# Products of phi(K) and V on eight small tiles of the matrix engine, with the memory kept as two heads per partition

## The chip, the cores and the metric

One core of a Trainium2 chip runs the kernel. The metric is the time of one execution on the device in microseconds (us). TensorE (PE in the profile) multiplies matrices into PSUM banks; VectorE (DVE), ScalarE (ACT) and GpSimd (POOL) work element by element; SyncE (SP) issues the transfers. Each engine works through a queue of its own, in order, and waits on semaphores for the others.

## The reference

Two branches work on the same input x (2048 rows of 512) and are mixed by a gate. Branch A is an attention with a compressive memory: 32 heads of 16 dimensions, four segments of 512 rows. Branch B is a gated feed-forward layer of width 1792.

```python
for s in range(N):                       # N = 4 segments, L = 512 rows each
    qs, ks, vs = q[:, :, s], k[:, :, s], v[:, :, s]
    p = softmax(einsum('bhqd,bhkd->bhqk', qs, ks) * scale + mask)
    a_dot = einsum('bhqk,bhkd->bhqd', p, vs)
    pq = phi(qs)                         # phi(t) = t + 1 for t > 0, else exp(t)
    num = einsum('bhld,bhde->bhle', pq, M)
    den = einsum('bhld,bhd->bhl', pq, z)[..., None] + 1e-06
    outs.append(g * num / den + (1.0 - g) * a_dot)
    pk = phi(ks)
    M = M + einsum('bhld,bhle->bhde', pk, vs)
    z = z + einsum('bhld->bhd', pk)
a = concat(outs) @ wo
b = (gelu(x @ w_gate) * (x @ w_up)) @ w_down
out = gate * a + (1 - gate) * b          # gate = sigmoid(sum(x * gate_w))
```

The memory M of a head is a 16x16 matrix and z a vector of 16; the program carries them together as 17 columns, since V is stored with a column of ones behind each head's 16.

## The kernel before

Everything is laid out by one program text that emits the instructions of all engines in order. The attention goes by blocks i = 8 heads of one segment (four chunks c per segment, 16 blocks in all). A block is visited several times, 72 visits in all (written `visits`). A visit emits the scores of one or two 64-key pieces (`group_qk`, L638: 4 or 8 matmuls on tiles of 32 rows by 128 columns), the exponential of the whole four-bank score tile on ScalarE (L643), and the mask of the diagonal on GpSimd (L647). Only one score tile exists, so the scores of the next visit wait for the exponential of this one. When all pieces of a block are there, `lump` emits the sum of values `pv` (L663): 128 loads and matmuls on eight tiles of 64 rows by 32 columns into two banks called od, which VectorE transposes out (L670) and later normalizes.

Between the scores of two visits TensorE is filled with units of the other work: projections k, q, v (L376, L290, L414), gate, up and down of branch B (L473, L494, L510), the output product (L527), and the memory. The units stand in streams; a planner (`fill_to`) picks the next one by its due visit and by VectorE's backlog, and adds up booked times: `t_pe` for TensorE, `t_act` for ScalarE. `left()` sums the booked TensorE times of units still to come, and the slack that follows from it is spread over the visits. A unit ends with the evacuation of its PSUM bank by VectorE or ScalarE. All these units and od share a pool of four banks (`gen`); `room_for_bank` finishes an open unit once two more banks have been taken.

The memory runs through these steps for each of the first three segments:

- `u_pk` (L406): a transposing transfer from SyncE turns phi(K) of a chunk so that the 512 keys stand on partitions (tile pk).
- `u_M` (L540): a unit, twice per segment, each for two chunks. For a chunk and each of four groups of 128 keys a full 128x128 load of pk is multiplied with V of all eight heads of the chunk, 8 x 17 = 136 columns (L548), into tile MT. So all 64 pairs of heads in a chunk are computed, of which the eight on the diagonal are used. VectorE adds MT to Macc (L555): 128 partitions (head and dimension) by 4 chunks by 8 heads by 17.
- `u_mask` (L559): a product with the block mask bm makes the bf16 tiles Mz (the denominators' part, L572) and Mn (L561, in two halves, two and eight visits later) of the next segment.
- `u_den` (L580, tile zd) and `mem_num` (L613, tile mn) multiply phi(Q) with them.

The units of the memory stand in one stream M, with due visits:

```python
us += [unit(u_M(s, half), NP * s + 10 + 2 * half, ("M", s),
            lambda s=s: count(("pk", s)) == NC8 and clock[0] >= pk_at[s] + 3)
       for half in range(2)]
us.append(unit(u_mask(s + 1), 0))
```

The turned keys of the next segment are written over the old ones, so `u_pk` of segment s + 1 waits for both halves of segment s. At the end a test of the inputs' size either leaves the result or runs `general()`, a slower safe path that the inputs here don't take.

Of the kernel before, what the change touches and what calls it, by code (L numbers as in the profile page):

```python
# [11 lines left out]
ALU = mybir.AluOpType  # L12

P = 128
D = 512
H = 32
DH = 16
NSEG = 4
DFF = 1792
FC = D // P  # L20
NC8 = H // 8
# [7 lines left out]
NP = 2 * NV  # L29
# [3 lines left out]
F32 = dt.float32  # L33
# [20 lines left out]
def kernel(  # L54
# [15 lines left out]
    nc = tc.nc  # L70
    S = A_x.shape[1]
    L = S // NSEG
    KT = L // P
# [10 lines left out]
    def const(shape, dtype, name):  # L84
        return cpool.tile(shape, dtype, name=name, tag=name)
# [10 lines left out]
    bm = const([P, 8, 17], BF, "bm")  # L96
# [1 line left out]
    beta = const([P, H], BF, "beta")  # L98
    gh = const([P, H], F32, "gh")
    og = const([P, H], F32, "og")  # L100
    Macc = const([P, NC8, 8, 17], F32, "Macc")
    Mn = [const([P, NC8, 128], BF, f"Mn{i}") for i in range(2)]
    Mz = [const([P, NC8, 8], BF, f"Mz{i}") for i in range(2)]
    rdm = [const([P, KT, H], F32, f"rdm{i}") for i in range(2)]
# [20 lines left out]
    def gen(name):  # L125
        return pgen.tile([P, 512], F32, name=name, tag="gen")
# [200 lines left out]
    def count(key):  # L327
        return done.get(key, 0)
# [208 lines left out]
            return MM512  # L537
        return 4 * MM512, EVAC, f

    def u_M(s, half):  # L540
        def f():
            T = gen("MT")
            Tv = T[:, 0:272].rearrange("p (c h e) -> p c h e", c=2, h=8)
            Tm = T[:, 0:272].rearrange("q (c j p e) -> q c j p e", c=2, j=4, p=2)
            for cc in range(2):
                c = 2 * half + cc
                for kt in range(KT):
                    nc.tensor.matmul(Tm[:, cc], lhsT=pk[:, kt, c * P:(c + 1) * P],  # L548
                                     rhs=Vh[s % 2][:, kt, :, 4 * c:4 * c + 4, 0:17]
                                     .rearrange("q p j e -> q j p e"),  # L550
                                     start=(kt == 0), stop=(kt == KT - 1))
                if cc == 0:
                    yield 0.3
            mv = Macc[:, 2 * half:2 * half + 2, :, :]
            nc.vector.tensor_tensor(out=mv, in0=mv, in1=Tv, op=ALU.add)  # L555
            return 0.3
        return 0.6, 0.4, f

    def u_mask(s):  # L559
        def half(h0):  # L560
            nc.vector.tensor_tensor(  # L561
                out=Mn[s % 2][:, h0:h0 + 2, :].rearrange("p c (h e) -> p c h e", h=8),
                in0=Macc[:, h0:h0 + 2, :, 0:16],
                in1=bm[:, None, :, 0:16].to_broadcast((P, 2, 8, 16)), op=ALU.mult)
            passed(0.0, 0.78)
            done["Mn", s] = count(("Mn", s)) + 1

        def f():
            if general_now[0]:
                half(0)  # L570
                half(2)
            nc.vector.tensor_tensor(out=Mz[s % 2][:, :, :], in0=Macc[:, :, :, 16],  # L572
                                    in1=bm[:, None, :, 16].to_broadcast((P, NC8, 8)),
                                    op=ALU.mult)
            if not general_now[0]:
                later(2, lambda: half(0))
                later(8, lambda: half(2))
        return 0.0, 0.2, f
# [123 lines left out]
    def unit(u, want, key=None, when=None):  # L702
        return u + (key, when, want)
# [8 lines left out]
    def passed(pe, dve=0.0):  # L712
        backlog[0] = max(0.0, backlog[0] - pe) + dve
        t_pe[0] += pe
# [18 lines left out]
    def room_for_bank():  # L733


        if current:
            current[0][3][0] += 1
            while current and current[0][3][0] > 2:
                step()
# [42 lines left out]
    def run(u):  # L782
        if u[0] == 0.0:
            u[2]()
        else:
            for _ in u[2]():
                pass
# [65 lines left out]
    us = []  # L853
    for s in range(NSEG - 1):
        us += [unit(u_pk(s, c), 0, ("pk", s), lambda s=s, c=c: ("k", s, c - c % 2) in ready
                    and (s == 0 or count(("M", s - 1)) == 2)) for c in range(NC8)]
    streams.append(Stream("T", us))

    def u_x3():
# [9 lines left out]

    us = []  # L870
    for s in range(NSEG - 1):
        us += [unit(u_M(s, half), NP * s + 10 + 2 * half, ("M", s),
                    lambda s=s: count(("pk", s)) == NC8 and clock[0] >= pk_at[s] + 3)
               for half in range(2)]
        us.append(unit(u_mask(s + 1), 0))
        us += [unit(u_den(s + 1, pair), NP * s + 16 + 9 * pair, ("den", s + 1),
                    lambda s=s, pair=pair: ("q", s + 1, 2 * pair) in ready)
               for pair in range(2)]
# [43 lines left out]
    def lump(i):  # L922
        s, c = i // NC8, i % NC8
        assert count(("vs", s)) == 1
        oT = oTs[s]
        o2 = wk2.tile([P, 16, 2, DH], BF, name="o2", tag="o2")
        room_for_bank()
        room_for_bank()
        oq = pv(s, c, blocks.pop(i))
        passed(PV_T, 1.44)  # L930

        def f_norm(p):
            norm(c, p, oq[p], o2)
            passed(0.0, 0.76)

        def f_back():
            back(c, o2, oT)
            passed(0.0, 0.7)
            if s == 0:
                later(1, f_ready)  # L940

        def f_add():
            assert (s, c) in tms
            add_mem(s, c, oT)
            passed(0.0, 0.43)
            later(1, f_ready)

        def f_ready():
            done["tr", s] = count(("tr", s)) + 1
        later(1, lambda: f_norm(0))  # L950
        later(2, lambda: f_norm(1))
        later(3, f_back)
        if s > 0:
            later(4, f_add)
# [131 lines left out]
    def general():  # L1086
        general_now[0] = True
        queue[0] = nc.gpsimd
        nc.gpsimd.memset(Macc[:, :, :, :], 0.0)
        nc.vector.tensor_copy(hm[:, :], bm[:, :, 16])  # L1090
        for s in range(NSEG):
            oT = wk2.tile([P, FC, L], BF, name="oT", tag="oT")
            oTs[s] = oT
            if s % NX == 0:
                rows = G[(s + 1) % NG][:, 0:KT, :]
                nc.gpsimd.dma_start(rows, x2[s * L:(s + 1) * L, :]
                                    .rearrange("(k p) d -> p k d", p=P))
                for fc in range(FC):
                    turn(xS[s % NX][:, fc, :].rearrange("p (k t) -> p k t", k=KT),
                         rows[:, :, fc * P:(fc + 1) * P])  # L1100
            for c in range(NC8):
                run(u_k(s, c))
                run(u_q(s, c))
            for kt in range(KT):
                run(u_v(s, kt))
            run(u_vz(s))
            run(u_vs(s))
            if s > 0:
                for c in range(0, NC8, 2):
                    phi_now(pq[:, c:c + 2, :], QT[:, c:c + 2, :])  # L1110
                run(u_mask(s))
                run(u_den(s, 0))
                run(u_den(s, 1))
            neg = G[(s + 1) % NG][:, 8, 0:P]
            nc.gpsimd.memset(neg, 0.0)
            nc.gpsimd.affine_select(out=neg, in_=neg, pattern=[[-1, P]], compare_op=ALU.is_ge,
                                    fill=-1e9 * DH ** 0.5, base=0, channel_multiplier=1)
            for c in range(NC8):
                o2 = wk2.tile([P, 16, 2, DH], BF, name="o2", tag="o2")
                if s > 0:  # L1120
                    mem_num(s, c)
                tiles = {}
                for b in range(5):
                    t = ptp.tile([P, 4, 512], BF, name="pT", tag="pT")
                    tiles[b] = (t, 0)
                    if 1 <= b <= 3:
                        tiles[NB - b] = (t, L - 64 * b)
                general_blocks(s, c, tiles)
                oq = pv(s, c, tiles)
                for p in range(2):  # L1130
                    norm(c, p, oq[p], o2)
                back(c, o2, oT)
                if s > 0:
                    add_mem(s, c, oT)
            for hs in range(HS):
                run(u_gate(s, hs, False))
            gelu(s)
            for hs in range(HS):
                run(u_up(s, hs))
            for qt in range(KT):  # L1140
                run(u_down(s, qt))
            for qt in range(KT):
                run(u_out(s, qt))
            if s < NSEG - 1:
                for c in range(0, NC8, 2):
                    phi_now(ktb[:, c:c + 2, :], ktb[:, c:c + 2, :])
                for c in range(NC8):
                    run(u_pk(s, c))
                for half in range(2):
                    run(u_M(s, half))  # L1150

    flag = nc.alloc_registers("safe", engines=[mybir.EngineType.PE, mybir.EngineType.DVE,
                                               mybir.EngineType.Activation,
# [36 lines left out]
```

## Time and profile before

| what | before |
|---|---|
| median of 3 runs (269.92 to 272.15) | 269.92 us |
| the profiled execution | 269.92 us |
| its span, first to last instruction | 268.2 us |
| mean granted TensorE clock | 0.999 of full speed |
| visits of the attention | 28.1 us (first scores) to 251.4 us (end of the last exponential) |
| the six pieces of u_M start at | 57.2, 62.8, 118.9, 127.2, 190.3, 196.1 us |

A page of the profile gives for each engine its busy time, its share of the span and its number of instructions. A row of a group gives the source line, the engine, the operation, output and inputs with their shapes (partitions x elements) and the count; behind the bar stand the busy time in all (us), the mean of one (ns), and the engine's idle time just before them with what ended it. Matmuls overlap, so a matmul's mean is its latency, and its cost is the distance from its start to the next one's. PEld are weight loads. A list of waits gives: who waited, for whom, us in total, how often, the longest. In order of time a row gives the start (us), the duration (us), engine, line, and the number of instructions merged.

### The profile page before, as it was taken

To read this page: it belongs to the slowest core of one execution; us is meant where nothing else is said; L and a number is where in the kernel's file an instruction comes from. 1 tells how busy PE (TensorE), PEld (TensorE's weight loads), DVE (VectorE), ACT (ScalarE), POOL (GpSimd) and SP (SyncE) were. 2 spreads that over 40 slices of the span, in tenths; PEclk is the share of its full clock that TensorE was granted. 3 is DMA by queue.
4 is the path that set the end of the run, shared out by engine and by line. 5 is a ranking of instruction groups with operands and counts; after the bars stand their busy time and mean duration, and the time that the engine had idled before them with its cause. 6 is when DMAs were issued, how large, how long until landed. Compare 5 with 4: busy or idle time off the path is not lost.

```text
span 268.2 us, 6580 instructions
## 1 busy us (share of the span) xinstructions
PE 262.7 (98%) x2713; PEld 118.0 (44%) x2713; DVE 204.0 (76%) x391; ACT 209.0 (78%) x163; POOL 156.9 (58%) x298
## 2 busy tenths in 40 slices
PE   7999999999999999999999999999999999999994
PEld 3454434344454444544444444434454544344441
DVE  2999575968778787697985979686889479698364
ACT  3236889999997998889999988889888987657510
POOL 4000158897905979987921998596785079655500
PEclk9999999999999999999999999999999999999999
DMA  6999911200070000301032001100000200003102
GB/s 213 304 197 329 341 36 39 42 4 0 20 145 2 0 22 22 78 4 42 0 61 62 4 21 42 42 20 22 20 24 21 66 2 20 2 20 42 40 22 83
DMA packets 30281, 16.59 MB, mean 62 GB/s; under 512 B 20008, under 2 KB 28968, under 8 KB 30248
## 3 DMA queue, kind: packets, MB, share of 16 engines
q1 hardware_dynamic: 30248, 16.14, 23.4%
q8 instruction: 22, 0.36, 0.6%
q14 instruction: 11, 0.09, 0.1%
HBM read 8.14 MB, written 2.10 MB: 38 GB/s over the span
## 4 chain that ended last, share of the span: by engine, by line
PE 87%; POOL 5%; issue 4%; DMA 2%; ACT 1%; SPq 0%; DVE 0%; ACTq 0%; DVEq 0%; POOLq 0%
PE gT L473 19%; PE uT L494 17%; PE dT L510 14%; PE lg L638 8%; PE od L663 6%; PE aT L527 5%; PE qT L290 5%; PE kT L376 5%; PE vT L414 4%; POOL pT L647 3%; POOL KTm L386 2%; DMA wk<-in_A_wk_dram 2%; PE MT L548 1%; PE mn L617 1%; ACT pT L643 1%
## 5 line engine op out<-in xcount | busy, mean ns | idle before, releaser
L647 POOL TENSOR_SCALAR_AFFINE_SELECT pT<-pT 64x256 bf16<-64x256 bf16 x256 | 113.9, 445 | 94.3 <-ACT pT L643 81.5
L643 ACT ACTIVATE pT<-lg 128x2048 bf16<-128x2048 f32 x72 | 135.1, 1876 | 24.9 <-PE lg L638 21.6
L494 PE MATMUL uT<-x,wup 128*128 128x512 bf16 x224 | 60.4, 380 | 0.0
L473 PE MATMUL gT<-x,wga 128*128 128x512 bf16 x224 | 57.0, 380 | 0.0
L510 PE MATMUL dT<-wdn,G 128*128 128x512 bf16 x224 | 52.9, 380 | 0.0
L500 DVE TENSOR_TENSOR G<-uT,G 128x512 bf16<-128x512 f32 x56 | 38.1, 684 | 6.4 <-PE uT L494 6.2
L386 POOL TENSOR_SCALAR KTm<-ktb,eo 128x512 bf16<-128x512 bf16 x26 | 40.6, 1571 | 1.3
L670 DVE STREAM_TRANSPOSE oq<-od 128x512 f32<-128x512 f32 x32 | 21.0, 695 | 19.3 <-PE od L663 19.3
L510 PEld LDWEIGHTS <-G 128*128 128x128 bf16 x224 | 20.8, 98 | 25.0 <-issue 2.1
L473 PEld LDWEIGHTS <-wga 128*128 128x128 bf16 x224 | 20.4, 98 | 23.9 <-issue 2.2
L494 PEld LDWEIGHTS <-wup 128*128 128x128 bf16 x224 | 19.8, 97 | 24.0 <-issue 5.4
L638 PE MATMUL lg<-QT,KTm 32*128 32x192 bf16 (+7 forms) x512 | 28.6, 287 | 0.0
L313 DVE CAST G<-gT 128x512 bf16<-128x512 f32 x24 | 16.5, 688 | 9.7 <-PE gT L473 9.5
L638 PEld LDWEIGHTS <-KTm 32*128 32x128 bf16 x512 | 8.3, 92 | 28.3 <-issue 28.0
L663 PE MATMUL od<-pT,V 64*32 64x128 bf16 (+7 forms) x512 | 19.4, 284 | 0.2 <-POOL pT L647 0.2
L663 PE MATMUL od<-pT,Vs 64*32 64x128 bf16 (+7 forms) x512 | 19.4, 284 | 0.0
L488 ACT ACTIVATE G<-G 128x3584 bf16<-128x3584 bf16 x6 | 18.8, 3182 | 0.0
L676 DVE SCALAR_TENSOR_TENSOR o<-oq,ogs,rden 128x256 bf16<-128x256 f32 x32 | 17.0, 532 | 1.1
L376 PE MATMUL kT<-x,wk 128*128 128x512 bf16 x64 | 16.8, 380 | 0.7 <-DMA wk<-in_A_wk_dram 0.7
L290 PE MATMUL qT<-x,wq 128*128 128x512 bf16 x64 | 16.6, 379 | 0.0
L532 DVE SCALAR_TENSOR_TENSOR tB<-aT,gct,tB 128x512 bf16<-128x512 f32 x16 | 11.9, 746 | 6.0 <-PE aT L527 5.7
L527 PE MATMUL aT<-wo,oT 128*128 128x512 bf16 x64 | 16.5, 380 | 0.0
(96 smaller groups left out, 276.0 us busy)
## 6 DMA issues: line engine op xcount, KB each, us to landing
out_dram<-tB SPq DMA_DIRECT2D x16, 128.0 KB, 1.7
wup<-in_B_w_up_dram SPq DMA_DIRECT2D x1, 1792.0 KB, 8.7
wdn<-in_B_w_down_dram SPq DMA_DIRECT2D x1, 1792.0 KB
wga<-in_B_w_gate_dram SPq DMA_DIRECT2D x1, 1280.0 KB, 10.5
Vs<-V SPq DMA_DIRECT2D x8, 144.0 KB, 2.6
G<-in_A_x_dram SPq DMA_DIRECT2D x2, 256.0 KB, 2.8
wk<-in_A_wk_dram SPq DMA_DIRECT2D x2, 256.0 KB, 4.5
wq<-in_A_wq_dram SPq DMA_DIRECT2D x1, 512.0 KB, 5.8
```

Of the source, the lines that this page charges most:

```text
L290: nc.tensor.matmul(T[:, :], lhsT=wq[:, fc, c * P:(c + 1) * P], rhs=xS[s % NX][:, fc, :], start=(fc == 0), stop=(fc == FC - 1))
L376: nc.tensor.matmul(T[:, :], lhsT=wk[:, fc, c * P:(c + 1) * P], rhs=xS[s % NX][:, fc, :], start=(fc == 0), stop=(fc == FC - 1))
L386: eng.tensor_scalar(out=KTm[:, (NC8 * s + c) % NK, :, p, :], in0=ktb[:, c, :].rearrange("q (b k) -> q b k", b=NB), scalar1=eo[:, p:p + 1], ...
L473: nc.tensor.matmul(T[:, :], lhsT=wga[:, fc, hs * P:(hs + 1) * P], rhs=xS[s % NX][:, fc, :], start=(fc == 0), stop=(fc == FC - 1))
L494: nc.tensor.matmul(T[:, :], lhsT=wup[:, fc, hs * P:(hs + 1) * P], rhs=xS[s % NX][:, fc, :], start=(fc == 0), stop=(fc == FC - 1))
L500: nc.vector.tensor_tensor(out=g, in0=T[:, :], in1=g, op=ALU.mult)
L510: nc.tensor.matmul(T[:, :], lhsT=G[s % NG][:, hs, qt * P:(qt + 1) * P], rhs=wdn[:, hs, :], start=(hs == 0), stop=(hs == HS - 1))
L527: nc.tensor.matmul(T[:, :], lhsT=oT[:, fc, qt * P:(qt + 1) * P], rhs=wo[:, fc, :], start=(fc == 0), stop=(fc == FC - 1))
L638: nc.tensor.matmul(lg[:, j, off:off + n], lhsT=KTm[rows, i % NK, b].rearrange("r p k -> r (p k)"), rhs=QT[rows, i % NC8, 64 * b:L], start= ...
L643: nc.scalar.activation(pT[:, :, :], lg[:, :, :], AF.Exp, scale=DH ** -0.5)
L647: nc.gpsimd.affine_select(out=v, in_=v, pattern=[[0, 4], [1, 64]], compare_op=ALU.is_ge, fill=0.0, base=0, channel_multiplier=-1)
L663: nc.tensor.matmul(od[p][32 * j:32 * j + 32, 64 * b:L], lhsT=w[:, 18 * h:18 * h + 32], rhs=t[rows, j, off:off + n], start=(b == 0), stop=( ...
```

## The change

The unit u_M is gone. A function `memory(s)` does the products of a whole segment at once, on the eight 64x32 tiles that `pv` uses: tile column j of a chunk holds its heads 2j and 2j + 1 (32 partitions), tile row `half` holds 64 of the 128 keys. Each load is 64 keys by 32 columns of pk, each matmul has the 2 x 17 = 34 columns of the same two heads, and the two halves of the keys go to two banks. That makes 128 loads and matmuls per segment in place of 16 full ones. VectorE adds both banks to Macc, which now keeps two heads per partition (4 x 2 x 17 values). `u_mask` spreads them to the four pairs while it masks, chunk by chunk for Mn; Mz comes first in both paths. `memory` isn't a unit of a stream: `lump` calls it, when the keys are turned, just ahead of `pv`, after two more calls of `room_for_bank`, and books 0.5 us of TensorE and 0.6 us of VectorE for it.

```diff
-    Macc = const([P, NC8, 8, 17], F32, "Macc")
+    Macc = const([P, NC8, 2, 17], F32, "Macc")
...
-    def u_M(s, half):
-        def f():
-            T = gen("MT")
-            Tv = T[:, 0:272].rearrange("p (c h e) -> p c h e", c=2, h=8)
-            Tm = T[:, 0:272].rearrange("q (c j p e) -> q c j p e", c=2, j=4, p=2)
-            for cc in range(2):
-                c = 2 * half + cc
-                for kt in range(KT):
-                    nc.tensor.matmul(Tm[:, cc], lhsT=pk[:, kt, c * P:(c + 1) * P],
-                                     rhs=Vh[s % 2][:, kt, :, 4 * c:4 * c + 4, 0:17]
-                                     .rearrange("q p j e -> q j p e"),
-                                     start=(kt == 0), stop=(kt == KT - 1))
-                if cc == 0:
-                    yield 0.3
-            mv = Macc[:, 2 * half:2 * half + 2, :, :]
-            nc.vector.tensor_tensor(out=mv, in0=mv, in1=Tv, op=ALU.add)
-            return 0.3
-        return 0.6, 0.4, f
+    def memory(s):
+        Ts = [gen("MT") for half in range(2)]
+        for c in range(NC8):
+            for kt in range(KT):
+                for j in range(4):
+                    for half in range(2):
+                        rows = slice(64 * half, 64 * half + 64)
+                        nc.tensor.matmul(
+                            Ts[half][32 * j:32 * j + 32, 34 * c:34 * c + 34]
+                            .rearrange("q (p e) -> q p e", p=2),
+                            lhsT=pk[rows, kt, P * c + 32 * j:P * c + 32 * j + 32],
+                            rhs=Vh[s % 2][rows, kt, :, 4 * c + j, 0:17],
+                            start=(kt == 0), stop=(kt == KT - 1),
+                            tile_position=(64 * half, 32 * j))
+        for half in range(2):
+            nc.vector.tensor_tensor(
+                out=Macc[:, :, :, :], in0=Macc[:, :, :, :],
+                in1=Ts[half][:, 0:34 * NC8].rearrange("q (c p e) -> q c p e", c=NC8, p=2),
+                op=ALU.add)
+        done["M", s] = 1
 
     def u_mask(s):
         def half(h0):
+            for c in (h0, h0 + 1):
+                nc.vector.tensor_tensor(
+                    out=Mn[s % 2][:, c, :].rearrange("q (j p d) -> q j p d", j=4, p=2),
+                    in0=Macc[:, c, None, :, 0:16].to_broadcast((P, 4, 2, DH)),
+                    in1=bm[:, :, 0:16].rearrange("q (j p) d -> q j p d", j=4), op=ALU.mult)
+            passed(0.0, 0.6)
...
-                    and (s == 0 or count(("M", s - 1)) == 2)) for c in range(NC8)]
+                    and (s == 0 or count(("M", s - 1)) == 1)) for c in range(NC8)]
...
-        us += [unit(u_M(s, half), NP * s + 10 + 2 * half, ("M", s),
-                    lambda s=s: count(("pk", s)) == NC8 and clock[0] >= pk_at[s] + 3)
-               for half in range(2)]
-        us.append(unit(u_mask(s + 1), 0))
+        us.append(unit(u_mask(s + 1), 0, None, lambda s=s: count(("M", s)) == 1))
...
         room_for_bank()
         room_for_bank()
+        for z in range(NSEG - 1):
+            if (count(("M", z)) == 0 and count(("pk", z)) == NC8 and clock[0] >= pk_at[z] + 3):
+                room_for_bank()
+                room_for_bank()
+                memory(z)
+                passed(0.5, 0.6)
         oq = pv(s, c, blocks.pop(i))
```

## The prediction

> **What bounds the kernel now.** I read the busy times first, then TensorE's waits, then the groups of the lines that the change touches, then TensorE in order of time around the work that is moved.
>
> ```profile
> PE 262.7 (98%) x2713; PEld 118.0 (44%) x2713; DVE 204.0 (76%) x391; ACT 209.0 (78%) x163; POOL 156.9 (58%) x298
> ```
>
> ```profile
> PE warm L166 <- PEq L1174: 1.0, 1, 1.0
> PE kT L376 <- DMA wk<-in_A_wk_dram: 0.7, 1, 0.7
> PE od L663 <- POOL pT L647: 0.2, 1, 0.2
> ```
>
> The second fence is the whole list of TensorE's waits: 1.9 us, of which 1.7 lie in the first 7 us. A busy TensorE is not one at its peak, so I also looked at the distance from one matmul's start to the next: matmuls of 512 columns start 216 ns apart all through the span, and hardly anything lies between them. So TensorE's own queue sets the end: what the change takes from it or adds to it is paid nearly one to one, and what it does to other engines costs nothing until TensorE waits for it. The groups that matter (count, total and mean ns):
>
> ```profile
> L548 PE MATMUL MT<-V,pk 128*128 128x136 bf16 x48 | 4.1, 226 | 0.0
> L588 PE MATMUL zd<-Mz,pq 128*128 128x8 bf16 x48 | 2.2, 167 | 0.0
> L555 DVE TENSOR_TENSOR Macc<-Macc,MT 128x272 f32<-128x272 f32 x6 | 2.5, 422 | 0.0
> L561 DVE TENSOR_TENSOR Mn<-Macc,bm 128x256 bf16<-128x256 f32 x6 | 3.1, 518 | 0.0
> L572 DVE TENSOR_TENSOR Mz<-Macc,bm 128x32 bf16<-128x32 f32 x3 | 0.8, 283 | 0.1
> ```
>
> The mean of a matmul row is its latency, with its neighbours overlapped. Its price is the distance between starts, read from TensorE in order of time (start us, duration us):
>
> ```profile
> 62.83 0.68 PE L548 MATMUL MT<-V,pk 128*128 128x136 bf16 x8
> 63.35 0.38 PE L494 MATMUL uT<-x,wup 128*128 128x512 bf16 x1
> ...
> 75.64 0.34 PE L588 MATMUL zd<-Mz,pq 128*128 128x8 bf16 x8
> 75.84 1.24 PE L473 MATMUL gT<-x,wga 128*128 128x512 bf16 x5
> ```
>
> Eight MT matmuls take 63.35 - 62.83 = 0.52 us (by the trace's nanoseconds 0.51). Eight zd matmuls, of 8 columns only, take 0.20 us, 25 ns each.
>
> **What is removed.** Six halves of u_M at 0.51 us: 3.07 us of TensorE. This is the most that the change can save there, 1.1% of the span.
>
> **What is added to TensorE.** Three calls of memory, each of 4 x 4 x 4 x 2 = 128 loads of 64x32 and 128 matmuls of 34 columns, in 16 groups of eight tiles. No row has that form; the nearest is od at L663, which runs on the same eight tiles. Its weight loads in order of time, first at the start of a sum of values, then at its end:
>
> ```profile
> 56.13 0.09 PEld L663 LDWEIGHTS <-V 64*32 64x32 bf16 x1 [0.21 <-issue]
> 56.13 0.09 PEld L663 LDWEIGHTS <-Vs 64*32 64x32 bf16 x1
> ...
> 56.18 0.09 PEld L663 LDWEIGHTS <-V 64*32 64x32 bf16 x1
> ...
> 57.05 0.09 PEld L663 LDWEIGHTS <-V 64*32 64x32 bf16 x1
> 57.06 0.09 PEld L663 LDWEIGHTS <-Vs 64*32 64x32 bf16 x1
> 57.07 0.09 PEld L663 LDWEIGHTS <-V 64*32 64x32 bf16 x1
> 57.07 0.09 PEld L663 LDWEIGHTS <-Vs 64*32 64x32 bf16 x1
> 57.08 0.09 PEld L663 LDWEIGHTS <-V 64*32 64x32 bf16 x1
> ```
>
> At the start 16 loads come within 0.05 us, 3.3 ns apart, with their matmuls between them: they stood ready. At the end, where the groups get short (128, then 64 columns), the last five come 8.3 ns apart, in each of the first six sums, which I looked at in nanoseconds. I read this as the pace at which new pairs of load and matmul reach the array once those that stood ready are used up; the longer groups before hide it (a group of 192 columns lasts 83 ns, eight pairs at 8.3 ns need 66). Memory is 128 such pairs with nothing long between them. Its bounds: below, 16 groups at 27 ns (eight pairs at 3.3 ns), 0.43 us; above, every one of the 128 matmuls at the 25 ns of a zd matmul, 3.2 us. I take the row of the same tiles: two groups standing ready at 27 ns and 14 at 66 ns, 0.98 us. Three calls: 2.94 us.
>
> [...]
>
> **What is moved.** The six pieces of u_M stood between units of the fillers (57.2, 62.8, 118.9, 127.2, 190.3 and 196.1 us). Now each call stands in front of an od, and two calls of room_for_bank more finish the open unit first. In the built order that puts one u_up matmul at visit 11, three at 29 and one at 52 between the scores and MT. A change of tile form costs about 0.10 us, from the last column of one form to the first matmul of the next (scores to full array 96 ns, full to scores 99, scores to od 91, od to full 104). Over the 72 visits the order has 162 such changes before and 164 after: +0.20 us.
>
> **The banks.** MT and od together now take all four banks of the generic pool, so od's second tile needs the bank of the u_up unit just ahead. Count from the start of that unit's last matmul: it ends at 0.38 us, the multiplication at L500 starts about 0.04 later, takes 0.68 and is seen at 1.14. MT starts at 0.216 + 0.10 = 0.32 and ends its issue at 1.30. So 0.16 us of cover; behind od's first pair all of TensorE's queue waits if VectorE is later than that. Ahead of this multiplication VectorE's built order has work that is due earlier, so I put nothing. od itself finds no pairs standing ready: its first group at 8.3 in place of 3.3 ns is 8 x 5 ns = 0.04 us, 0.12 for three.
>
> **VectorE.** Two adds of 136 columns replace two of 272: by the slope between Mz and Mn (235 ns over 224 columns, 1.05 ns each) 422 - 143 = 0.28 us each, 0.85 us saved in all. Mn becomes 12 instructions of 128 columns for 6 of 256: 283 + 96 x 1.05 = 0.38 us, 4.6 for 3.1. Net +0.65 us on an engine with 64 us idle, hidden beside TensorE; without that cover it costs 0.65. The adds stand ahead of od's two transposes and run while od computes (0.98 us). SyncE: some pk transposes trade places with Vs copies; a pk transpose lands 2.5 us after issue, and its user comes three visits (7.8 us) later at the earliest. GpSimd clears a smaller Macc at the start, under the loads. TensorE waits for none of these.
>
> **The sum.** -3.07 + 2.94 + 0.20 + 0.12 = +0.19 us. The profiled execution took 269.92 us for a span of 268.2, 1.7 us lie outside it; the median shown is 269.92 too. Forecast: 270.1 us, no change that counts.
>
> **The rivals.**
> (a) The pairs come at 3.3 ns throughout: MT 0.43 us. For it: the 16 loads at 56.13, and the program's own planner, which books 0.5 us. Then od would be ready at 0.75 us, and the bank wait takes its place until 1.14: MT with its wait is 0.82 us, three are 2.46, and the sum -3.07 + 2.46 + 0.20 = -0.41: 269.5. Did the bank not bind: -3.07 + 1.30 + 0.20 = -1.57, 268.4.
> (b) Slower: a short matmul costs its 25 ns whatever its tile. Place: the three MT blocks. 128 x 25 ns = 3.2 us each, 9.6 for three; sum -3.07 + 9.6 + 0.20 = +6.7: 276.6. It decides from 15 ns per matmul on (1.9 us a block, 2.8 us more in all). For it: zd's rows. Against it: od's 64-column group, whose eight matmuls start within 0.03 us. [...]
> (c) The planner loses six units of 0.6 us from its book of work and lays visits 3 to 59 anew. Now TensorE arrives at the scores only 0.05 to 0.6 us after the previous exponential's end in most visits. If the new order is short by 0.05 us a visit, 57 visits give +2.9 us: 273. Against it: the units are the same, the order from visit 60 on is the same, and the same book filled every visit before.
> That the change doesn't do what it says is out: the built order has three blocks of 128 MT matmuls.
>
> **How the numbers follow.** Chances: forecast 0.63, (a) 0.18, (b) 0.07, (c) 0.12. 1% is 2.7 us, about what a measurement of this kernel can tell from no change. Faster by over 1% needs nearly all of the 3.07 us: 0.02. Slower: (b) and somewhat over half of (c): 0.14. Range: from 268.8, with the bound case and some of the unbound one in (a), to 272.8, short of (b) and of half of (c).
>
> **What would show it.** Right: MT from its first start to od's first in 0.9 to 1.1 us, loads about 8 ns apart after the first groups; no new line among TensorE's waits over 0.3 us; Mn at about 0.38 us. Loads 3.3 ns apart with a wait of od for DVE L500 mean (a); MT blocks of 2 us or more (b); waits at L643 for ACT (c). A span that is off by over 2 us with MT at 1 us would make the prediction wrong.

## The result, and the profile after

| | before | after |
|---|---|---|
| median | 270.03 us (269.75 to 272.15, 8 runs) | 272.76 us (272.31 to 272.98, 8 runs) |
| ratio to before | | 1.0095, 95% interval [1.0078, 1.0112] |
| the profiled execution, its span | 269.92, 268.2 us | 272.98, 271.1 us |

The changed kernel is 0.95% slower: 2.7 us above the forecast of 270.1, inside its range of 268.8 to 272.8 but at its upper end. Single runs stand apart from their kernel's others by about as much (272.15 of the eight before, up to 272.23 in later series, one of the ten of experiment 3 at 272.46); no trace of one is kept, so whether they have the same cause is open. The page of the changed kernel begins so (span and busy times):

```profile
span 271.1 us, 7262 instructions
PE 262.3 (97%) x3049; PEld 117.9 (43%) x3049; DVE 202.7 (75%) x397; ACT 208.5 (77%) x163; POOL 157.6 (58%) x298
```

TensorE is busy 0.4 us less than before and the span is 2.9 us longer, so the loss is no work of TensorE. Nor is it a wait of TensorE in the middle. This is the whole list of TensorE's waits after:

```profile
PE kT L376 <- DMA wk<-in_A_wk_dram: 1.6, 1, 1.6
PE warm L166 <- PEq L1181: 1.0, 1, 1.0
PE od L668 <- POOL pT L652: 0.2, 1, 0.2
```

There is no new line. The wait for the weights wk at the start is 0.9 us longer in this execution. The first wait of kT, for wk or for VectorE's x, moves from execution to execution (0.4 to 1.6 us), and the first scores start between 27.8 and 28.5 us in the profiled executions that add no more than 69 instructions to VectorE.

To find the rest I cut the span in three at two events that every kernel has: the first matmul of the scores and the last matmul of the output product (their starts, from the trace):

| us | before | after | difference |
|---|---|---|---|
| start of the span to the first scores | 28.06 | 28.51 | +0.46 |
| first scores to the last output matmul | 236.28 | 236.33 | **+0.05** |
| last output matmul to the end (the tail below) | 3.85 | 6.28 | **+2.43** |

All of the attention, with everything that the change edits, takes as long as before. The loss stands behind the last matmul, in code that the diff doesn't touch. There, each of TensorE, ScalarE and VectorE reads the flag of the safe path and jumps over `general()`, and SyncE waits for all of them. SyncE's wait for VectorE's jump, in the list of SyncE's waits, before:

```profile
SPq L1185 <- DVEq L1160: 0.5, 1, 0.5
```

and after (the same two lines of the program text, seven further down):

```profile
SPq L1192 <- DVEq L1167: 3.1, 1, 3.1
```

By the trace, VectorE's load of the flag takes as long in both, 548 and 543 ns. The branch itself starts 84 ns behind the instruction ahead of it before and 461 ns after; from its start to VectorE's next instruction pass 602 ns before and 2829 ns after. ScalarE and TensorE jump in 458 to 462 ns in both. In those 2.8 us almost nothing moves on the transfer queues; here the window from VectorE's branch to its next instruction, after (packets, MB, share of 16 engines):

```profile
DMA packets 43, 0.06 MB, mean 21 GB/s; under 512 B 16, under 2 KB 40, under 8 KB 40
...
q8 instruction: 1, 0.02, 3.3%
q1 hardware_dynamic: 40, 0.02, 2.8%
q14 instruction: 2, 0.02, 2.3%
```

q8 and q14 are the queues that this view calls instruction. Two packets of 8192 bytes on q14 start 0.58 and 0.69 us behind the branch. In the kernel before no such fetch starts between the branch and VectorE's next instruction.

The step that was forecast is there as well. TensorE in order of time around the first block of memory, after (start, duration):

```profile
56.38 0.39 PE L494 MATMUL uT<-x,wup 128*128 128x512 bf16 x1
56.70 1.19 PE L547 MATMUL MT<-V,pk 64*32 64x34 bf16 x128
57.71 0.38 PE L668 MATMUL od<-pT,V 64*32 64x512 bf16 x1
```

From MT's first start to od's are 1.01 us; the three blocks take 1.014, 1.066 and 1.015. The first 32 pairs come 3.3 ns apart, but for two steps of 10 to 16 ns; then there is one gap of 92 ns, and from there every pair takes 8.3 ns. The second block has two further steps of 34 ns, which make it longer. The first weight loads of od stand at the same pace:

```profile
57.70 0.09 PEld L668 LDWEIGHTS <-V 64*32 64x32 bf16 x1
57.71 0.09 PEld L668 LDWEIGHTS <-Vs 64*32 64x32 bf16 x1
57.72 0.09 PEld L668 LDWEIGHTS <-V 64*32 64x32 bf16 x1
```

The groups of the changed lines, after (total us, mean ns | idle before):

```profile
L564 DVE TENSOR_TENSOR Mn<-Macc,bm 128x128 bf16<-128x128 f32 x12 | 3.6, 342 | 0.0
L547 PE MATMUL MT<-V,pk 64*32 64x34 bf16 x384 | 3.6, 184 | 0.0
L555 DVE TENSOR_TENSOR Macc<-Macc,MT 128x136 f32<-128x136 f32 x6 | 1.8, 296 | 1.8 <-PE MT L547 1.5
L572 DVE TENSOR_TENSOR Mz<-Macc,bm 128x32 bf16<-128x32 f32 x3 | 0.6, 193 | 0.0
```

So two theories stood against each other. **J**: the loss is the jump at the end, and what decides it is the place of VectorE's branch in VectorE's own queue; the change moves it by adding five instructions to VectorE. **W**: it comes from the changed work itself, such as the new order, the new Macc, or what it leaves behind. The place is counted in the built program, every instruction of VectorE from its first to the branch: 444 before, 449 after.

### The profile page after: what moved, and what is told of

It is laid out like the page before. It is cut to its first block, busy times and chain, and to the rows that moved or that the text cites. A ratio compares the mean times of both kernels' runs of the same rounds, so it can differ in the third digit from the quotient of the medians.

```text
span 271.1 us, 7262 instructions
## 1 busy us (share of the span) xinstructions
PE 262.3 (97%) x3049; PEld 117.9 (43%) x3049; DVE 202.7 (75%) x397; ACT 208.5 (77%) x163; POOL 157.6 (58%) x298
## 4 chain that ended last, share of the span: by engine, by line
PE 86%; POOL 5%; issue 4%; DMA 2%; ACT 1%; SPq 0%; DVE 0%; ACTq 0%; DVEq 0%; POOLq 0%
PE gT L473 18%; PE uT L494 17%; PE dT L510 14%; PE lg L643 8%; PE od L668 6%; PE aT L527 5%; PE qT L290 5%; PE kT L376 5%; PE vT L414 4%; POOL pT L652 3%; POOL KTm L386 2%; DMA wk<-in_A_wk_dram 2%; PE MT L547 1%; PE mn L622 1%; ACT pT L648 1%
## 5 line engine op out<-in xcount | busy, mean ns | idle before, releaser
L500 DVE TENSOR_TENSOR G<-uT,G 128x512 bf16<-128x512 f32 x56 | 38.1, 683 | 12.1 <-PE uT L494 11.9
L313 DVE CAST G<-gT 128x512 bf16<-128x512 f32 x23 | 15.7, 683 | 5.4 <-PE gT L473 5.2
L668 PE MATMUL od<-pT,Vs 64*32 64x64 bf16 (+7 forms) x512 | 19.4, 284 | 0.0
L532 DVE SCALAR_TENSOR_TENSOR tB<-aT,gct,tB 128x512 bf16<-128x512 f32 x16 | 11.8, 738 | 6.2 <-PE aT L527 5.9
```

What stands on the lines that cost most here:

```text
L500: nc.vector.tensor_tensor(out=g, in0=T[:, :], in1=g, op=ALU.mult)
L668: nc.tensor.matmul(od[p][32 * j:32 * j + 32, 64 * b:L], lhsT=w[:, 18 * h:18 * h + 32], rhs=t[rows, j, off:off + n], start=(b == 0), stop=( ...
```

## The experiments

**1. The kernel before, with five idle instructions on VectorE.** Nothing of the memory is changed; five one-column memsets of an unused tile stand at the start of the program.

```diff
     load_inputs()
+    pad = const([P, 64], F32, "pad")
+    for i in range(5):
+        nc.vector.memset(pad[:, i:i + 1], 0.0)
```

> The kernel before with five clears of one column each added on VectorE at the very start, where it waits for the first transposed inputs. They bring VectorE's queue from 443 to 448 instructions ahead of the branch that skips the safe path, as in the changed kernel; nothing of the memory is changed. Theory J (the jump): the changed kernel loses 2.4 us in VectorE's jump over the safe path at the end, because of where the branch stands in the queue. It expects 272.4 us, with 2.7 us from the branch to VectorE's next instruction. Theory W (the work): the loss belongs to the products on small tiles and to the order laid anew. It expects 270.0 us.

Measured: 272.68 us (272.42 to 272.77), ratio 1.0095 [1.0075, 1.0114]: the same loss as the changed kernel's, with none of its work. SyncE's wait for the jump:

```profile
SPq L1188 <- DVEq L1163: 3.1, 1, 3.1
```

The branch starts 460 ns behind its forerunner, the next instruction 2806 ns behind the branch; first scores to last output matmul 236.27 us, the tail 6.26 us. This is J.

**2. The control: three in place of five.** The branch at place 447.

> The kernel before with three such clears: 446 instructions of VectorE ahead of the branch. A control for what clears cost by themselves. Theories J and W both expect 270.0 us (0.6 us from the branch to VectorE's next instruction); if J is right but the border lies lower than 448, 272.4 us.

Measured: 270.01 us, 0.9998 [0.9988, 1.0008]; 581 ns behind the branch, tail 3.86 us. So it isn't that instructions are added, but how many.

**3. The changed kernel with its branch moved on.** The same lines in the changed kernel with `range(16)`: place 465.

> The changed kernel with sixteen such clears: the branch moves on from place 449 to 465 of VectorE's queue, nothing else changes. Theory J with a narrow bad zone behind a border at 448: 270.3 us, the jump back at 0.6 us. J with all places behind 448 bad, or theory W: 272.8 us, told apart by the jump's length in the trace.

Measured: 270.36 us (269.52 to 272.46), 1.001 [0.9987, 1.0032]; 627 ns behind the branch, tail 3.88 us, MT blocks of 1.015, 1.067 and 1.016 us as in the changed kernel, first scores to last output matmul 236.30 us. Its page, and its SyncE's wait for the jump:

```profile
span 268.6 us, 7278 instructions
PE 263.5 (98%) x3049; PEld 118.7 (44%) x3049; DVE 203.2 (76%) x413; ACT 208.6 (78%) x163; POOL 157.1 (58%) x298
```

```profile
SPq L1195 <- DVEq L1170: 0.5, 1, 0.5
```

The loss is gone with all of the changed work in place. W has nothing left to explain: the change to the memory costs nothing that these runs can tell from zero, and the forecast of 270.1 us fits the kernel without the jump's loss.

**4. Memory on four tiles of 128 rows by 32 columns.** If the block's price is pairs times pace, half the pairs should take about half of it. Here all 128 keys of a group are one load: 64 pairs in place of 128, one bank, one add.

```diff
     def memory(s):
-        Ts = [gen("MT") for half in range(2)]
+        T = gen("MT")
...
-                    for half in range(2):
-                        rows = slice(64 * half, 64 * half + 64)
-                        nc.tensor.matmul(
-                            Ts[half][32 * j:32 * j + 32, 34 * c:34 * c + 34]
-                            .rearrange("q (p e) -> q p e", p=2),
-                            lhsT=pk[rows, kt, P * c + 32 * j:P * c + 32 * j + 32],
-                            rhs=Vh[s % 2][rows, kt, :, 4 * c + j, 0:17],
-                            start=(kt == 0), stop=(kt == KT - 1),
-                            tile_position=(64 * half, 32 * j))
+                    nc.tensor.matmul(
+                        T[32 * j:32 * j + 32, 34 * c:34 * c + 34]
+                        .rearrange("q (p e) -> q p e", p=2),
+                        lhsT=pk[:, kt, P * c + 32 * j:P * c + 32 * j + 32],
+                        rhs=Vh[s % 2][:, kt, :, 4 * c + j, 0:17],
+                        start=(kt == 0), stop=(kt == KT - 1),
+                        tile_position=(0, 32 * j))
...
```

> The changed kernel with the products of the memory on four tiles of 128 rows by 32 columns: 64 loads and matmuls per segment in place of 128, one bank and one add of VectorE in place of two; all else alike. VectorE's branch stands at place 444, as before. If pairs of load and matmul are fed at 8.3 ns each once those that stand ready are used up, a block goes from 1.01 to some 0.5 us, and no bank has to wait for the unit just ahead. MT to od changes the tile form, 0.1 us each. Theory J: 268.9 us (before 270.0, -3.07 + 1.5 + 0.5). Theory W: 272.8 - 1.2 = 271.6 us. If a block stays near 1 us, the feeding isn't by the pair, and J gives 270.3 us.

Measured: 268.56 us (268.53 to 268.73), 0.9947 [0.9928, 0.9966], faster than both kernels. TensorE in order of time:

```profile
55.86 0.39 PE L494 MATMUL uT<-x,wup 128*128 128x512 bf16 x1
56.18 0.67 PE L545 MATMUL MT<-V,pk 128*32 128x34 bf16 x64
56.77 0.39 PE L665 MATMUL od<-pT,V 64*32 64x512 bf16 x1
```

From MT's first start to od's first: 0.595, 0.622 and 0.596 us, of which the last 0.10 is a change of form from 128x32 to 64x32 that the eight-tile kernel doesn't have (its od starts 8 to 9 ns behind the last pair). The pairs alone take 0.48, 0.51 and 0.48 us from first to last. They are made up otherwise than the eight-tile blocks: the first 32 come in fours, about 25 ns from one four to the next and so 6 to 7 ns a pair, no gap of 92 ns follows, and the rest come at about 8.4 ns. First scores to last output matmul: 234.92 us, 1.4 us under the changed kernel's; the blocks account for 1.28 of it (3.095 - 1.813). The branch stands at 444 and costs 603 ns.

**5. Where the loss lies.** The kernel before with other numbers of memsets, each moving VectorE's branch to another place. Nine: place 453.

> The kernel before with nine clears on VectorE at the start: its branch stands at place 453. Places 444, 447 and 465 gave a jump of 0.6 us, 449 one of 2.8. If the slow places are only the first one or two behind 448: 270.0 us and 0.6 us; if they reach further: 272.5 us and 2.8 us.

Sixty-nine: place 513.

> The kernel before with 69 clears: branch at place 513, the first behind 512 = 8 x 64. If the border comes every 64 places: 272.5 us and a jump of 2.8 us, plus what 69 clears cost at the start (they run while VectorE waits for its first work, some 4 us; up to 1 us if they do not fit). If the border at 448 is of another kind: 270.0 us and 0.6 us.

Both together: 453 costs 1139 ns behind the branch (270.94 us, 1.002 [0.9996, 1.0044]) and 513 costs 628 ns (270.02 us, 0.9999 [0.998, 1.0019]). So the loss is down to 0.5 us at 453, four places behind 449, and gone at 465 (627 ns); and 513, 64 places behind 449, doesn't have it.

**6. The branch's place or the target's?** Five memsets again, and 30 more inside `general()`, which is built and jumped over: the branch stays at 449, the place that it jumps to lies 30 instructions further.

> The kernel before with the five clears of e1 and thirty more inside the safe path, which is not run: the branch stays at place 449, the jump's target moves 30 places on. If the place of the branch decides: 272.6 us and 2.8 us as in e1. If the place of the target decides: 270.0 us and 0.6 us.

Measured: 272.49 us, 1.009 [1.0055, 1.0124]; 3013 ns behind the branch. The branch's place decides it, at least for these two targets.

**7. The period and the exact border.** Four memsets (448, between the good 447 and the bad 449), 133 (577, which is 449 + 128) and 261 (705, which is 449 + 256). The last two delay the start: 133 and 261 memsets at 29 ns ahead of VectorE's first useful work.

> VectorE's branch at place 448, the last place between the good 447 and the bad 449. It says on which side the border lies: 0.6 us behind the branch and 270.0 us in all, or 2.8 us and 272.7 us; I expect the good side.

> VectorE's branch at place 577 of its queue (449 + 128; the fetches in the traces are 8192 bytes each). If the loss comes back every 128 places: 2.8 us from the branch to VectorE's next instruction, 6.2 us from the last output matmul's start to the end of the span. If the period is longer than 128 places or there is none: 0.6 us and 3.9 us, as at 513. The memsets at the start may delay the first scores by some us; that part is read apart, the first scores to the last output matmul stays 236.3 us.

> VectorE's branch at place 705 (449 + 256). If the loss comes back every 256 places: 2.8 us behind the branch and a tail of 6.2 us; if it does not: 0.6 and 3.9 us. The start is later by the memsets (261 at 29 ns, 7.6 us, less what VectorE waits there anyway), which is read apart.

SyncE's wait for the jump at 448, at 577 and at 705, one fence each:

```profile
SPq L1188 <- DVEq L1163: 0.5, 1, 0.5
```

```profile
SPq L1188 <- DVEq L1163: 3.2, 1, 3.2
```

```profile
SPq L1188 <- DVEq L1163: 3.3, 1, 3.3
```

All runs of the series, by the place of VectorE's branch:

| place | kernel | branch behind the instruction ahead, ns | next instruction behind the branch, ns | tail, us | median, us |
|---|---|---|---|---|---|
| 444 | before | 84 | 602 | 3.85 | 270.03 |
| 447 | before + 3 | 85 | 581 | 3.86 | 270.01 |
| 448 | before + 4 | 85 | 570 | 3.86 | 269.77 |
| **449** | after | 461 | 2829 | 6.28 | 272.76 |
| **449** | before + 5 | 460 | 2806 | 6.26 | 272.68 |
| **449** | before + 5, target + 30 | 460 | 3013 | 6.47 | 272.49 |
| 453 | before + 9 | 85 | 1139 | 4.58 | 270.94 |
| 465 | after + 16 | 85 | 627 | 3.88 | 270.36 |
| 513 | before + 69 | 84 | 628 | 3.88 | 270.02 |
| **577** | before + 133 | 460 | 2903 | 6.36 | 274.66 |
| **705** | before + 261 | 460 | 3063 | 6.52 | 279.10 |

(The medians of the last two rows are of two runs each, and their totals also hold 1.7 and 6.8 us of later first scores, beside the after's 28.51; first scores to last output matmul is 236.3 us in every row.) In these runs the border lies between 448 and 449 and comes back 128 and 256 places on: a branch at 449, 577 or 705 starts 0.38 us later and pays 2.2 to 2.5 us more behind it, one at 453 pays 0.5 us more, and those at 444, 447, 448, 465 and 513 lie within 0.06 us of each other (570 to 628 ns).

The fetches on q14 fit a reading, which is inferred and not shown: that a packet is one stretch of 128 places. From its 8192 bytes that makes an estimated 64 bytes an instruction. With the branch at 448 no packet comes near it until 1.2 us later. With the branch at 453 one comes 0.70 us ahead of the branch, when VectorE has just crossed the border, and the next 0.96 us behind it. At 449 two come 0.58 and 0.69 us behind the branch, and VectorE goes on only 2.2 us after the first. The reading is that the crossing starts a fetch of its own and that a jump within it waits for that fetch; no view shows such a wait itself, only these times.

Two more places in the traces fit this reading. With the branch at 465 a packet on q14 starts 8.3 us ahead of the branch, and with the branch at 513 one starts 40 us ahead, at times when the kernel before has none; both are over long before the jump. And with the branch at 453 it isn't the branch that starts late but the instruction that stands at place 449 there, the last one of L532: 415 ns behind the end of its wait, against 45 or 46 ns for the same instruction in every other run. With the branch at 465, where the packet has come before VectorE starts place 449, the branch starts 85 ns behind its forerunner. So in these runs the branch is 0.38 us late on 449, 577 and 705, and the last instruction of L532 is 0.37 us late on 449; and the jump is long from 449, 577 and 705 (2.8 to 3.1 us) and less so from 453 (1.1 us).

That a long piece of code is jumped over doesn't decide it: all kernels here jump over the safe path, which is 1680 or more instructions of VectorE, and the runs show 0.6 or 2.8 us by the branch's place.

**8. Four tiles behind the sum of values.** With one bank, `memory` can stand behind od, where the order has fewer changes of form, and without the two extra calls of `room_for_bank`. The tiles are those of experiment 4; the other edit against the changed kernel is:

```diff
+        oq = pv(s, c, blocks.pop(i))
+        passed(PV_T, 1.44)
         for z in range(NSEG - 1):
             if (count(("M", z)) == 0 and count(("pk", z)) == NC8 and clock[0] >= pk_at[z] + 3):
-                room_for_bank()
-                room_for_bank()
                 memory(z)
-                passed(0.5, 0.6)
-        oq = pv(s, c, blocks.pop(i))
-        passed(PV_T, 1.44)
+                passed(0.5, 0.3)
```

> The products on four tiles of 128x32 as in e4, but behind the sum of values instead of in front of it and without finishing the open unit first. Per block the forms now go scores, od, MT, full array (three changes) in place of scores, full, MT, od, full (four); the kernel before had two at this place. VectorE's branch stands at place 443. By 0.10 us a change, three fewer than e4: 268.25 us. If the changes are not what e4 still pays, 268.6 us as e4; if od's transposes come late for the MT bank or MT waits, above 268.6 us.

Measured: 268.80 us (268.54 to 269.12), 0.9952 [0.9936, 0.9969]: no better than the version of experiment 4. The changes of form fell from 171 to 169, but od to MT takes 119 ns, MT's first start to the next u_up matmul 0.62 to 0.65 us, the pairs alone 0.50 to 0.53 against 0.48 to 0.51, and in two places the unit behind shows a gap of about 116 ns. The two versions' intervals overlap. Of the expected three changes two were saved, 0.2 us; these longer stretches are of that size.

## Why the prediction was right, and where it was wrong

- **The work that the change edits: right.** The sum said +0.19 us; first scores to last output matmul went by +0.05, and in the changed kernel with the branch moved (experiment 3) by +0.02. That kernel's 270.36 us stands against the forecast of 270.1. With the blocks as they were measured (3.10 us in place of 2.94) the same sum gives +0.35; where the 0.3 us between went is open.
- **The price of a block: right.** 0.98 us forecast, 1.01, 1.07 and 1.02 measured, with the pace of 8.3 ns that was read from the end of od. The make-up differed: four groups came at 3.3 ns a pair, not two, and a gap of 92 ns follows them, which the sum did not have; these nearly cancel. Experiment 4 supports the price by the pair: half the pairs take about half the time (0.48 us), and behind the first 32 the pace is about the same (8.4 against 8.3 ns).
- **Rivals (a) and (b) are out.** The pairs at 3.3 ns throughout would have made 0.43 us a block, 25 ns for each of the 128 matmuls 3.2 us; the blocks took 1.01, 1.07 and 1.02.
- **The banks: right.** No wait of TensorE for VectorE's multiplication at L500 is in its list.
- **Changes of form: right** in number (two more in the traces too) and size: from the last u_up matmul to MT pass 320, 309 and 320 ns in the three blocks, against 216 from one u_up matmul to the next, so 0.09 to 0.10 us for the change (0.10 forecast).
- **VectorE: right that it is hidden, wrong in size.** Mn's instructions take 342 ns against 380 forecast, the adds 296 against 280, and Mz's, which the forecast left as they were, 193 against 283 before. Count times mean of the three groups is 6.5 us before and after, where +0.65 was forecast. VectorE's whole busy time fell from 204.0 to 202.7 us, so most of the fall lies in lines that the change doesn't edit; its cause is open.
- **Rival (c) has the size of the loss, but not its place.** It asked for 0.05 us in each of 57 visits and for waits at the scores. The visits are as long as before.
- **What failed: "The profiled execution took 269.92 us for a span of 268.2, 1.7 us lie outside it."** The sum was laid on this total as if everything but the named terms stayed. The 3.9 us between the last output matmul and the end were not opened at all, since no edited line lies in them. There "So TensorE's own queue sets the end" doesn't hold: SyncE waits for VectorE's jump. VectorE's added instructions were costed as busy time only, "hidden beside TensorE". What they did was to move the jump at the end by five places, over a border, for +2.4 us. The prediction named this case as its refutation: a span off by over 2 us with MT at 1 us. None of its rivals covers it. So the mechanism forecast for the edited work was right, but that the total of 272.76 us lies inside the range is luck: the upper end, 272.8, was set by (b) and (c), and neither came about.

## What to carry to other kernels

The number of instructions ahead of a jump can cost more than the instructions, here 2.4 us for five one-column memsets (experiment 1; in the run with 69 of them 60 take 1.72 us, 29 ns each): where a kernel ends with a branch over code that isn't run, look at the tail by itself in both profiles, and repeat the old kernel with the same number of idle instructions before a small loss is put down to the change. The blocks of small tiles on TensorE went here by their pairs of load and matmul: behind the first 32, 8.3 ns a pair on 64x32 and 8.4 ns on 128x32, with 34 columns each. So read the pace of the pairs from a group on the same tiles, and price such a block by it. Here the larger tile won: 64 pairs of 128x32 in place of 128 of 64x32 turned no gain into one of 0.5% (0.9947, [0.9928, 0.9966]).

## What the runs showed of the hardware that was not expected

- A jump on VectorE took 0.57 to 0.63 us to the next instruction from places 444, 447, 448, 465 and 513 of its queue, 1.1 us from 453, and 2.8 to 3.1 us from 449, 577 and 705. The branch itself starts 0.38 us late at 449, 577 and 705, and in the run with the branch at 453 the instruction at 449 starts 0.37 us late. Why the place matters is inferred from the fetches and not settled.
- Pairs of load and matmul on the eight 64x32 tiles start 3.3 ns apart for the first 32 pairs, then stop for 92 ns, and then go at 8.3 ns a pair, for 34 columns here as for the last loads of od. On four tiles of 128x32 (experiment 4) the first 32 pairs take 6 to 7 ns each, without the stop, and the rest 8.4 ns.
